# Order of the small row pieces in the second layer of a sparse expert kernel

## The chip, the cores and the metric

The kernel runs on one core of a Trainium2 chip. The metric is device time in microseconds (us) of one execution; lower is better. Three executions of the kernel before took 378.6, 380.12 and 380.73 us; the median, 380.12 us, is the time before.

## The reference

A linear attention without softmax is followed by a layer of eight experts. Each of 4608 rows (8 sequences of 576) has 512 features (8 heads of 64).

```python
kv  = einsum('bhsd,bhse->bhde', k, v)
out = einsum('bhsd,bhde->bhse', q, kv)
x   = out / sqrt(mean(out*out, -1) + 1e-6) * g_norm     # then (B,H,S,D) -> (4608, 512)

do_compute = x @ w_skip > 0                             # other rows are passed through
logits = x[do_compute] @ w_gate                         # 8 experts
e      = argmax(logits);  gate = softmax(logits)[e]
h      = maximum(x @ w1[e], 0)                          # 512 -> 1024
out    = x + gate * (h @ w2[e])                         # 1024 -> 512
```

All of it is in fp32. Each row that is computed goes through one expert alone, so the work is sparse: a row is gathered, taken through its expert's two layers, scaled and added to itself, and scattered back.

## The kernel before

**Stages.** The attention and the gating take roughly the first 130 us; the rest, up to 380 us, are the eight experts, ranked by their number of rows. Expert 0, the fullest, is begun beside the end of the attention. The others, 1 to 7, follow in one loop (`experts`), each with a first layer (`fast_1`) and a second layer (`fast_2`). Code behind a condition, for more rows than an expert has room for, isn't executed with these inputs.

**Rows and pieces.** The experts have room for 352, 352, 320, 288, 288, 288, 256 and 256 rows. Rows are cut into pieces of 128, and of what is left, 64 and 32. So from expert 1 on each has two whole blocks of 128 rows; expert 1 has a piece of 64 and one of 32 besides, expert 2 one of 64, experts 3, 4 and 5 one of 32, and experts 6 and 7 none.

**Seven products for two blocks.** The second layer of the two whole blocks is one matrix product, cut in 2 x 2 x 2 blocks and done with seven block products in place of eight (Strassen's method, in Winograd's form). Each product is four matmuls of 128 x 128 weights with 256 columns (line 1192); the profile shows each matmul as two rows, so a product is eight. Two PSUM banks, X and Y, hold the results, each in two halves, lo and hi:

1. X lo: block 0 of h with w2; ScalarE copies it out as p1 (`held`).
2. Y lo: sums of h with sums of w2; VectorE adds p1 to it (`add`, line 1196), then ScalarE copies it out as u (line 1202).
3. X hi: copied out by ScalarE as p5.
4. Y lo again, on top: it needs the add and the copy u of step 2 to be finished. VectorE then writes Y hi = Y lo + p5.
5. X lo again, on top.
6. X hi again, on top; VectorE adds u, and block 0's result is complete in X.
7. Y lo again, on top; block 1's result is complete in Y.

**Small pieces.** A piece of 64 or 32 rows goes the plain way (`layer_2`, line 1124). Its weights are only 64 or 32 columns wide, and two or four matmuls fill the array side by side: for each of the eight blocks f of 128 features there are 128/m matmuls of 512 m/128 columns, which write different partitions of one bank. A piece is in all 16 (m = 64) or 32 (m = 32) matmuls, twice that many rows in the profile. They accumulate in a bank of their own.

**Other work in the second layer.** VectorE makes, in twelve jobs given out by `do(work, n)`, what the next expert's first layer takes: four sums of its x (line 1140), then eight sums of its first-layer weights (line 1134). A finished piece goes to `put`, which is `result`: VectorE scales it with the gate and adds x (line 1336), and POOL issues an indirect DMA that scatters the rows (line 1339). In the first expert of the loop VectorE also has ten small instructions of a count of rounds and row tables ahead of these jobs.

**What sets the order.** Every engine's order is the order of the program text (`tc.manual_schedule`); no planner moves anything. Waits between engines come from the tiles' dependencies. PSUM banks come from a ring of seven (`bank`), claimed in program order. Weights are loaded on SP's queue, one expert's first and second layer (2 MB each) behind the other, into two sets of buffers; the load for expert r + 2 starts when expert r's weights were last read. Gathers and scatters are on POOL's queue; the gathers of expert r + 2 are issued at the start of expert r.

Of the kernel before, what the change touches and what calls it, by code (L numbers as in the profile page):

```python
# [17 lines left out]
def kernel(  # L18
# [58 lines left out]
    FC = F // 128  # L77
# [154 lines left out]
    for a in range(2):  # L232
        r = slice(a * 64, (a + 1) * 64)
# [215 lines left out]
    qTs, q8s, ops, rss, halves, lgs, xbs = {}, {}, {}, {}, {}, {}, {}  # L449
# [541 lines left out]
    with tc.tile_pool(name="wpool_b", bufs=1, reuse_waits="tile") as wpool_b, \  # L991
# [6 lines left out]
        def bank():  # L998
            return ps_b.tile([P, 512], FP32, tag="bank", name="bank")
# [116 lines left out]
        def layer_2(r, ht, piece, yps=None, fs=range(FC)):  # L1116

            off, m = piece[0:2]
            n = DM * m // P
            ht = ht if callable(ht) else (lambda f, all=ht: all[:, f, :])  # L1120
            yps = yps or bank()
            for f in fs:
                for q in range(P // m):
                    nc.tensor.matmul(out=yps[q * m:(q + 1) * m, 0:n], lhsT=ht(f)[:, off:off + m],  # L1124
                                     rhs=w_sb[r][1][:, f, q * n:(q + 1) * n],
                                     start=(f == 0), stop=(f == FC - 1), skip_group_check=True)
            return yps
# [15 lines left out]
        HF, HD = FC // 2, DC // 2  # L1143
# [40 lines left out]
        def do(work, n=None):  # L1184
            n = len(work) if n is None else min(n, len(work))
            for job in work[:n]:
                job()
            del work[:n]

        def product(out, k, lhsT, rhs, start):  # L1190
            for i in range(k):
                nc.tensor.matmul(out=out, lhsT=lhsT(i), rhs=rhs(i), start=start and i == 0,  # L1192
                                 stop=i == k - 1, skip_group_check=True)

        def add(to, x, y):
            nc.vector.tensor_tensor(out=to, in0=x, in1=y, op=ALU.add)  # L1196

        def held(x, tag):

            n = x.shape[-1]  # L1200
            t = ffn.tile([P, 256], FP32, tag=tag, name=tag)[:, 0:n]
            nc.scalar.copy(out=t, in_=x)  # L1202
            return t
# [61 lines left out]
        def fast_2(r, ht, rest, work, put, part=None):  # L1265

            w2, s, t = w_sb[r][1], sums.pop((r, "h")), sums.pop((r, "w2"))
            lo, hi = slice(0, HM), slice(HM, DM)

            def h(j, m):  # L1270
                return lambda f: ht[:, j * HF + f, m * P:(m + 1) * P]

            def hs(i):
                return lambda f: s[:, i, f, :]

            def w(j, ds):
                return lambda f: w2[:, j * HF + f, ds]

            def ws(i):
                return lambda f: t[:, i, f, :]  # L1280

            halves = [(piece, fs) for piece in rest for fs in (range(HF), range(HF, FC))]
            ys = {}

            def aside():
                if halves:
                    piece, fs = halves.pop(0)
                    if piece not in ys:  # L1290
                        ys[piece] = bank()
                    layer_2(r, ht, piece, ys[piece], fs)
                    if fs.stop == FC:
                        put(piece[0:2], ys[piece])

            X, Y = bank(), bank()
            product(X[:, lo], HF, h(0, 0), w(0, lo), True)
            p1 = held(X[:, lo], "p1")
            do(work, 4)
            product(Y[:, lo], HF, hs(1), ws(1), True)  # L1300
            add(Y[:, lo], Y[:, lo], p1)
            u = held(Y[:, lo], "u")
            do(work, 2)
            product(X[:, hi], HF, hs(0), ws(0), False)
            p5 = held(X[:, hi], "p5")
            do(work, 2)
            aside()
            product(Y[:, lo], HF, h(0, 1), ws(2), False)
            add(Y[:, hi], Y[:, lo], p5)
            if part:  # L1310
                part(1, 1, Y)
            do(work, 2)
            aside()
            product(X[:, lo], HF, h(1, 0), w(1, lo), False)
            do(work, 2)
            aside()
            product(X[:, hi], HF, hs(2), w(1, hi), False)
            add(X[:, hi], X[:, hi], u)
            put((0, P), X)
            aside()  # L1320
            product(Y[:, lo], HF, h(1, 1), ws(3), False)
            if part:
                part(1, 0, Y)
            else:
                put((P, P), Y)
            while halves:
                aside()
            do(work)

        def result(piece, yps, xg, tables, group):  # L1330
# [52 lines left out]
        def experts(pieces, widths, srcs, xt, ht, yps0, tables, group):  # L1383

            for r in range(E):
# [36 lines left out]
                if r == 0:  # L1422
                    if yps0 is None:
                        gather_all(2, pieces, *srcs)
                    ys = [bank() for _ in todo]
                    for fs in (range(HF), range(HF, FC)):
                        for piece, y in zip(todo, ys):
                            layer_2(r, ht, piece, y, fs)
                    do(beside, 4)
                    for piece, y in zip(todo, ys):  # L1430
                        result(piece, y, xgs[r], tables, group)
                    do(beside)
                else:
                    if yps0 is not None and r == 1:
                        rnd_i = rounds()
                    if yps0 is not None and r == E - 1:
                        n_rounds.append(nc.values_load(rnd_i[0:1, 0:1], min_val=1,
                                                       max_val=ROUNDS + 1))
                    of = {piece[0:2]: piece for piece in todo}
                    part = None  # L1440
                    if yps0 is not None and r == 1:
                        two = half_rows(tables[0][0])
                    if yps0 is not None and r == E - 1:
                        part = lambda c, half, y: half_result(c, half, y, xgs[r], two,
                                                              tables[0][1], group)
                    fast_2(r, ht, todo[2:], beside,
                           lambda key, y: result(of[key], y, xgs[r], tables, group), part)
# [134 lines left out]
```

## Time and profile before

| | us |
|---|---|
| median of three executions | 380.12 |
| profiled execution, in all | 381.81 |
| its span, first to last instruction | 380.0 |
| TensorE matmul busy | 365.3 (96%) |
| TensorE weight loads busy | 313.2 (82%) |
| VectorE busy | 245.1 (64%) |
| ScalarE busy | 142.3 (37%) |
| POOL busy | 124.2 (33%) |
| the seven products and the first layers, line 1192, share of the chain | 44% |
| small pieces, line 1124, share of the chain | 9% |

The granted TensorE clock is 0.999 of full speed throughout. In rows of the profile, "PE" is a matmul and "PEld" a weight load, which overlaps matmuls; "DVE" is VectorE, "ACT" ScalarE. A row in order of time gives start, length, engine, line, operation, output and inputs, shapes, and the number of merged instructions; the time in brackets is how long the engine was idle before and what ended it. [...] successive matmuls overlap, and it is the distance of their starts that counts. In the chain, and among the waits, "issue" is time in which an engine waited for nothing that the profile shows. A row of a table by stretches gives the stretch, its length, then the busy time (and number) of PE, PEld, DVE, ACT and POOL in it, the granted clock, and the DMA engines' share and GB/s. A row of waits gives who waited for whom, the time in total, how often, and the longest.

### The profile page before, as it was taken

What the parts mean: (1) busy time and instruction counts of PE and PEld (TensorE: products, weight loads), DVE (VectorE), ACT (ScalarE), POOL (GpSimd) and SP (SyncE); (2) the same over time, 40 slices, a digit from 0 to 9 for tenths busy, and PEclk for the clock granted to TensorE, in tenths of its full rate; (3) what the DMA queues carried; (4) which work ended last, traced back from release to release, by engine and by line L of the source; (5) the groups of instructions that cost most, each with busy time, mean ns of one, the idle gap of its engine ahead of it and who ended that gap; (6) DMA issues with size and microseconds to landing.
All of it is one profiled execution on the core that took longest, in us unless ns stands there. A gap on an engine that the chain in (4) does not pass through costs nothing.

```text
span 380.0 us, 9623 instructions
## 1 busy us (share of the span) xinstructions
PE 365.3 (96%) x3848; PEld 313.2 (82%) x3848; DVE 245.1 (64%) x626; ACT 142.3 (37%) x383; POOL 124.2 (33%) x195
## 2 busy tenths in 40 slices
PE   8999999999988998999999999999999999999994
PEld 4688797898977857779869987988988998998983
DVE  3344458667787961666756665875876876877831
ACT  2366676676774301214402430430440430431410
POOL 7025467655668544223013302212201211202003
PEclk9999999999999999999999999999999999999999
DMA  8999999996487738966516462672662762800001
GB/s 292 393 390 389 403 402 398 403 352 205 136 296 207 216 92 281 394 203 237 194 62 201 144 223 57 232 257 68 239 213 87 261 194 92 273 3 28 29 1 52
DMA packets 32039, 81.70 MB, mean 215 GB/s; under 512 B 2474, under 2 KB 2482, under 8 KB 31988
## 3 DMA queue, kind: packets, MB, share of 16 engines
q1 hardware_dynamic: 28176, 69.47, 52.1%
q0 software_dynamic: 3792, 11.53, 8.9%
q8 instruction: 32, 0.52, 0.6%
q14 instruction: 19, 0.16, 0.1%
q10 hardware_dynamic: 20, 0.02, 0.0%
HBM read 66.80 MB, written 14.48 MB: 214 GB/s over the span
## 4 chain that ended last, share of the span: by engine, by line
PE 84%; issue 6%; DVE 3%; ACT 3%; POOL 2%; DMA 1%; POOLq 0%; DVEq 0%; ACTq 0%
PE bank L1192 44%; PE bank L1124 9%; PE o_ps L496 6%; PE sum_ps L379 5%; PE bank L1112 4%; PE q_ps L460 3%; PE g_ps L393 2%; PE q_ps L170 2%; PE bank L1093 2%; DMA xg<-out_dram,src 1%; DVE rs L518 1%; DVE xl L537 1%; ACT sq L510 1%; PE q_ps L814 1%; PE g_ps L411 1%
## 5 line engine op out<-in xcount | busy, mean ns | idle before, releaser
L1202 ACT COPY p<-bank 128x128 f32<-128x128 f32 (+6 forms) x70 | 20.8, 297 | 100.3 <-PE bank L1192 89.3
L1192 PE MATMUL bank<-xt,w 128*128 128x128 f32 (+5 forms) x336 | 55.5, 288 | 0.1
L567 POOL TENSOR_TENSOR xb<-xl,g_b 128x512 f32<-128x512 f32 x36 | 44.4, 1234 | 32.5 <-DVE rs L532 30.6
L1192 PEld LDWEIGHTS bank<-xt,w 128*128 128x128 f32 x336 | 47.0, 190 | 2.0 <-DVE bank L1196 1.5
L1196 DVE TENSOR_TENSOR bank<-bank,p 128x128 f32<-128x128 f32 (+6 forms) x70 | 23.6, 337 | 37.1 <-PE bank L1192 36.0
L1192 PE MATMUL bank<-xs,s 128*128 128x128 f32 (+5 forms) x224 | 36.7, 289 | 0.0
L496 PE MATMUL o_ps<-kvd,qT 128*128 128x146 f32 x240 | 35.8, 290 | 1.0 <-ACT kvd L415 0.7
L1339 POOL DMA_INDIRECT out_dram<-xg,arows x9 | 10.0, 1112 | 78.7 <-DVE xg L1336 77.8
L518 DVE TENSOR_REDUCE rs<-sq 128x8 f32<-128x512 f32 x36 | 24.6, 682 | 16.2 <-ACT sq L510 16.0
L1124 PE MATMUL bank<-w,ht 128*32 128x128 f32 (+2 forms) x436 | 34.5, 319 | 0.0
L496 PEld LDWEIGHTS o_ps<-kvd,qT 128*128 128x128 f32 x240 | 31.6, 188 | 2.0 <-ACT kvd L415 1.5
L1192 PEld LDWEIGHTS bank<-xs,s 128*128 128x128 f32 x224 | 31.1, 190 | 1.0 <-ACT p L1202 0.8
L1339 POOL DMA_INDIRECT out_dram<-xg,rows x14 | 13.9, 994 | 53.2 <-DVE xg L1336 42.7
L1124 PEld LDWEIGHTS bank<-w,ht 128*32 128x32 f32 (+2 forms) x436 | 18.8, 120 | 13.2 <-issue 10.9
L537 DVE TENSOR_TENSOR xl<-o_ps,rs 128x584 f32<-128x584 f32 x34 | 26.1, 767 | 4.5 <-DVE rs L532 0.5
L1192 PE MATMUL bank<-t,ht 128*128 128x256 f32 x112 | 27.1, 385 | 0.0
L1192 PE MATMUL bank<-w,ht 128*128 128x256 f32 x112 | 27.1, 384 | 0.0
L1084 POOL DMA_INDIRECT xg<-out_dram,src x14 | 14.4, 1026 | 37.2 <-DMA out_dram<-xg,rows 13.9
L379 PE MATMUL sum_ps<-v,k 64*64 64x64 f32 x1152 | 25.6, 228 | 0.6 <-issue 0.6
L510 ACT ACTIVATE sq<-o_ps 128x512 f32<-128x512 f32 x34 | 20.3, 596 | 15.0 <-PE o_ps L496 14.5
L379 PEld LDWEIGHTS sum_ps<-v,k 64*64 64x64 f32 x1152 | 21.7, 140 | 4.7 <-issue 2.1
L1192 PE MATMUL bank<-t,hs 128*128 128x256 f32 x112 | 25.3, 379 | 0.0
(217 smaller groups left out, 680.5 us busy)
## 6 DMA issues: line engine op xcount, KB each, us to landing
w<-in_moe_w_dram SPq DMA_DIRECT2D x16, 2048.0 KB, 7.9
k<-in_k_dram SPq DMA_DIRECT2D x16, 576.0 KB, 9.7
v<-in_v_dram SPq DMA_DIRECT2D x16, 576.0 KB, 12.0
q<-in_q_dram SPq DMA_DIRECT2D x16, 576.0 KB, 9.2
out_dram<-xb SPq DMA_DIRECT2D x29, 256.0 KB, 4.4
out_dram<-xb POOLq DMA_DIRECT2D x7, 256.0 KB, 5.5
xg<-out_dram,src POOLq DMA_INDIRECT x16, 3.5
out_dram<-xg,rows POOLq DMA_INDIRECT x16, 7.1
```

The lines of the kernel that those rows point to most:

```text
L379: nc.tensor.matmul(out=sum_ps[w * 64:(w + 1) * 64, a, u, :], lhsT=kt[r, 2 * u + w, c, :], rhs=vt[r, 2 * u + w, c, :], start=(c == 0), stop ...
L496: nc.tensor.matmul(out=ps[:, w, 0:2 * PK].rearrange("p (r k) -> p r k", r=2)[:, :, cols], lhsT=qT[:, w, a, :], rhs=kvds[b % KVD][:, u, w, ...
L510: nc.scalar.activation(out=sq[:, :, :, :], in_=heads(ps, G, G + 2 * D), func=ACT.Square)
L518: nc.vector.tensor_reduce(out=rs[:, :, :], in_=sq[:, :, :, :].rearrange("p x y (a d) -> p x (y a) d", a=2), axis=AX.X, op=ALU.add)
L537: nc.vector.tensor_tensor(out=xl[:, :, :, :].rearrange("p x y (a k) -> p x (y a) k", a=2), in0=ps[:, :, 0:2 * PK].rearrange("p x (h k) -> ...
L567: late.append((lambda: nc.gpsimd.tensor_tensor(out=xb[:, :, 4 * u * D:(4 * u + 4) * D].rearrange("p r (w x) -> p r w x", w=2), in0=xl[:, : ...
L1112: nc.tensor.matmul(out=hps[:, cols], lhsT=w_sb[r][0][:, dc, f * P:(f + 1) * P], rhs=xt[:, dc, cols], start=(dc == 0), stop=(dc == DC - 1))
L1124: nc.tensor.matmul(out=yps[q * m:(q + 1) * m, 0:n], lhsT=ht(f)[:, off:off + m], rhs=w_sb[r][1][:, f, q * n:(q + 1) * n], start=(f == 0), s ...
L1192: nc.tensor.matmul(out=out, lhsT=lhsT(i), rhs=rhs(i), start=start and i == 0, stop=i == k - 1, skip_group_check=True)
L1196: nc.vector.tensor_tensor(out=to, in0=x, in1=y, op=ALU.add)
L1202: nc.scalar.copy(out=t, in_=x)
L1339: ins = nc.gpsimd.indirect_dma_start(out=cut_rows(m)[:, :], out_offset=bass.IndirectOffsetOnAxis(ap=rows[:, col:col + 1], axis=0), in_=x, ...
```

## The change

Before, each small piece was computed in two halves, four blocks f each. `aside()` took the next half, and stood at four places: between products 3 and 4, 4 and 5, 5 and 6, 6 and 7. Expert 1 used all four, the experts with one piece the first two. Afterwards all small pieces stand between products 6 and 7, each whole, one behind the other; `put` of each follows its last matmul, and so comes after block 0's. One of VectorE's twelve jobs, the last of the four x sums, moves from ahead of the add of product 2 to behind it. The first layers, expert 0, and the number and shapes of all instructions stay. Experts 6 and 7 have no small pieces: for expert 6 only the place of the x sum changes, for expert 7 nothing.

```diff
-            halves = [(piece, fs) for piece in rest for fs in (range(HF), range(HF, FC))]
-            ys = {}
-
-            def aside():
-                if halves:
-                    piece, fs = halves.pop(0)
-                    if piece not in ys:
-                        ys[piece] = bank()
-                    layer_2(r, ht, piece, ys[piece], fs)
-                    if fs.stop == FC:
-                        put(piece[0:2], ys[piece])
-
             X, Y = bank(), bank()
             product(X[:, lo], HF, h(0, 0), w(0, lo), True)
             p1 = held(X[:, lo], "p1")
-            do(work, 4)
+            do(work, 3)
             product(Y[:, lo], HF, hs(1), ws(1), True)
             add(Y[:, lo], Y[:, lo], p1)
             u = held(Y[:, lo], "u")
-            do(work, 2)
+            do(work, 3)
             product(X[:, hi], HF, hs(0), ws(0), False)
             p5 = held(X[:, hi], "p5")
             do(work, 2)
-            aside()
             product(Y[:, lo], HF, h(0, 1), ws(2), False)
             add(Y[:, hi], Y[:, lo], p5)
             if part:
                 part(1, 1, Y)
             do(work, 2)
-            aside()
             product(X[:, lo], HF, h(1, 0), w(1, lo), False)
             do(work, 2)
-            aside()
             product(X[:, hi], HF, hs(2), w(1, hi), False)
             add(X[:, hi], X[:, hi], u)
             put((0, P), X)
-            aside()
+            for piece in rest:
+                put(piece[0:2], layer_2(r, ht, piece))
             product(Y[:, lo], HF, h(1, 1), ws(3), False)
             if part:
                 part(1, 0, Y)
             else:
                 put((P, P), Y)
-            while halves:
-                aside()
             do(work)
```

## The prediction

> **What bounds the kernel now.** I read the page's chain of work first, because a change of order matters only on the engine that sets the end.
>
> ```profile
> PE 84%; issue 6%; DVE 3%; ACT 3%; POOL 2%; DMA 1%; POOLq 0%; DVEq 0%; ACTq 0%
> PE bank L1192 44%; PE bank L1124 9%; PE o_ps L496 6%; PE sum_ps L379 5%; PE bank L1112 4%; PE q_ps L460 3%; PE g_ps L393 2%; PE q_ps L170 2%; PE bank L1093 2%; DMA xg<-out_dram,src 1%; DVE rs L518 1%; DVE xl L537 1%; ACT sq L510 1%; PE q_ps L814 1%; PE g_ps L411 1%
> ```
>
> TensorE carries the chain. The two first lines are the two that the change reorders: L1192 are the seven products, L1124 the small pieces. Next I asked whether TensorE waits for anybody there (waits of its weight loads, 184 to 350 us).
>
> ```profile
> PEld bank L1124 <- issue: 4.0, 12, 0.3
> PEld bank L1192 <- issue: 3.1, 12, 0.4
> PEld bank L1192 <- DVE bank L1196: 1.1, 5, 0.3
> PEld bank L1192 <- ACT p L1202: 0.6, 4, 0.2
> ```
>
> Little of it is for other engines; 24 times, some 7 us in all, the next weights wait for "issue", which is nothing that the profile names. The order of time shows where: expert 3 (one 32-row piece), TensorE alone.
>
> ```profile
> 250.28 1.89 PE L1192 MATMUL bank<-w,ht 128*128 128x256 f32 x8
> 252.01 3.62 PE L1192 MATMUL bank<-t,hs 128*128 128x256 f32 x16
> 255.56 1.08 PE L1124 MATMUL bank<-w,ht 128*32 128x128 f32 x32
> 256.57 1.99 PE L1192 MATMUL bank<-t,ht 128*128 128x256 f32 x8
> 258.50 1.08 PE L1124 MATMUL bank<-w,ht 128*32 128x128 f32 x32
> 259.51 1.99 PE L1192 MATMUL bank<-w,ht 128*128 128x256 f32 x8
> ```
>
> Expert 6 has no small piece, so it already runs the seven products in the order of the new kernel:
>
> ```profile
> 338.69 3.62 PE L1192 MATMUL bank<-t,hs 128*128 128x256 f32 x16
> ...
> 340.69 0.43 DVE L1196 TENSOR_TENSOR bank<-bank,p 128x256 f32<-128x256 f32 x1 [1.02 <-PE bank L1192]
> ...
> 341.15 0.37 ACT L1202 COPY u<-bank 128x256 f32<-128x256 f32 x1 [1.89 <-DVE bank L1196]
> 341.93 1.70 PEld L1192 LDWEIGHTS bank<-t,ht 128*128 128x128 f32 x8
> 342.14 1.89 PE L1192 MATMUL bank<-t,ht 128*128 128x256 f32 x8
> ```
>
> Start to start a product there takes 1.73 us. In expert 3 a product between halves takes 1.93 (256.57 to 258.50): each visit to a small piece also slows its neighbours. The stretches from the first product of the second layer to the first of the next expert price this:
>
> ```profile
> 184.53:203.19 18.66, 18.66 (x155) 14.06 (x153) 11.84 (x33) 1.95 (x6) 2.21 (x2) 1.00 0.38 125
> 219.77:236.01 16.24, 16.24 (x91) 12.60 (x89) 9.79 (x21) 1.96 (x6) 1.24 (x2) 1.00 0.40 143
> 250.28:264.79 14.51, 14.51 (x122) 12.11 (x121) 9.62 (x21) 2.38 (x7) 1.24 (x2) 1.00 0.45 153
> 336.96:349.05 12.09, 12.09 (x58) 10.65 (x57) 9.26 (x20) 1.89 (x5) 0.03 (x1) 1.00 0.00 1
> ```
>
> The first number is the length, the next is PE busy: TensorE fills every one. Experts 1, 2, 3 and 6, in that order; 4 and 5 give 14.50 each. So the small pieces cost 6.57, 4.15, 2.42, 2.41 and 2.41 us over the bare 12.09.
>
> [...] In the single records of expert 3, in-mode starts of a product are 0.216 us apart; the last start before a piece is 0.309 before the piece's first one, 0.093 more. [...] the 32-wide matmuls do start in groups of four, within 0.02 us, a group every 0.109 us (64-wide: pairs every 0.216).
>
> **The change, part by part.**
>
> *Fewer visits.* The number of matmuls is the same; what falls away is mode switches. A 32-row half is 8 groups, 8 x 0.109 = 0.87 us, but costs 2.42 / 2 = 1.21: a visit's switches cost 0.335. A 64-row half is 8 pairs, 8 x 0.216 = 1.73, and costs 4.15 / 2 = 2.075: 0.345. Expert 1 confirms it: 2 x 1.73 + 2 x 0.87 = 5.20, plus 2 x 0.345 + 2 x 0.335 = 1.36, gives 6.56 against 6.57. Experts 3, 4, 5 drop one visit each of two: 3 x 0.335 = 1.0 us. Expert 2 drops one: 0.345.
>
> *Expert 1* has four visits, and afterwards goes from products to the 64-row piece, to the 32-row piece, to the product: three switches for eight. A direct switch from 64 to 32 is in no trace of before. From the records [...] a slower start in the new mode: 0.06 for 64, 0.04 for 32, 0.10 for 128 columns. Three switches make 0.28 + 0.20 = 0.48 for 1.36: 0.88 saved. Bounds: the direct switch free, 1.02; each piece paying a whole visit, 0.68. I take 0.88. A gain from it beyond that has no source, since no matmul goes.
>
> *The cover between products 3 and 4.* Product 4 adds to the half bank that product 2 wrote; VectorE must have added to it and ScalarE copied it to u. With the half piece gone, product 3's 1.73 us alone covers this. Expert 6 shows it enough: u is done at 341.52, the weights start at 341.93. Experts 2 to 5: in expert 3 u ends 254.85, product 4's weights would be due at 255.25; expert 4 is tightest, 284.52 against 284.57. Cost nothing; behind the waiting weight load all later matmuls would queue, so each us late there is a us of the end.
> Expert 1 is another matter. VectorE comes late there, since ten small instructions of the rounds count and the row tables run first; u ends at 189.98, and product 4's weights would be due at 189.50. Moving one of the four x sums (0.41 us from start to start) behind the add brings u to 189.58: 0.08 late, of which the 0.2 us between a weight load and its matmul may hide all. I take 0.05 us; 0 to 0.15. Left in place, it would have been 0.4.
>
> *The moved x sum* costs VectorE nothing: in experts 2 to 6 VectorE idles before that add (1.02 us in expert 6). Its taker is the next expert's first layer, over 8 us later. The two w sums behind it shift by the same 0.41; VectorE is busy 9.3 of 12.09 us in expert 6, done in time.
>
> *Scaled results and scatters.* Block 0's result, with its scatter, now goes first; the small ones follow, then block 1's. Each is one VectorE instruction (0.34 to 0.75) and one POOL issue (about 1.0). Between the end of the last small piece and block 1's result lie product 7 and its way, 1.73 + 0.2 + 0.75, so POOL is free again. The gathers of expert r + 2 stand behind block 1's scatter on POOL as before and are taken a whole expert (29 us) later. Cost nothing.
>
> *Banks, weights on SP's queue.* The pieces' banks are claimed in the same order, and come round seven claims later, some 6 us into the next first layer. The next second-layer weights load when TensorE last read the old ones: product 6 before (issue at 263.26), the end of the piece now. Both are one product before the stage's end, and 7.9 us of landing have an expert's time. Experts 6 and 7 keep their TensorE order.
>
> Sum: 1.0 + 0.345 + 0.88 - 0.05 = 2.18 us. The profiled execution has a span of 380.0 us and took 381.81 in all; after, 377.8 and 379.6. The median of the three runs is 380.12, near the span; the same 2.18 off it gives **377.9 us**, ratio 0.994. What a measurement of this kernel can tell from no change is about 0.5%, 1.9 us: the forecast lies only just beyond.
>
> **Rivals.**
> *Slower: long runs of small matmuls starve.* Place: the second half of each 32-row piece. [...] It decides from 44 ns per matmul (0.55 us in each of four experts eats the gain); 59 ns makes it slower by 0.5%. Against it stands a run of 80 matmuls in 64-by-64 tiles[...], with (1.40 - 0.23) / 79 = 15 ns each:
>
> ```profile
> 21.00 1.40 PE L379 MATMUL sum_ps<-v,k 64*64 64x64 f32 x80
> ```
>
> [...] Product 4 late in every expert with pieces, as expert 4's tight 0.05 us and expert 1's backlog suggest: 0.2 us in five experts leaves 1.2 of the gain, 379.0. Against it: 0.4 us to spare in experts 3 and 6.
>
> *Nothing saved.* The 0.33 belongs to the start of each accumulating half (its first weights), not to the visit, or the other experts' loads set the pace behind TensorE: 380.1. Against it: the product after a half also lengthens, and TensorE is busy in 100% of these stretches.
>
> **How the numbers follow.** Forecast 0.70, of which 0.10 falls inside the 0.5% by the scatter of medians (the three runs spread over 2.1 us); the wait 0.13, of which 0.01 beyond it; nothing saved 0.08; slower 0.09. Faster 0.61, within 0.30, slower 0.09. The forecast's own bounds are a saving of 1.9 to 2.4, 377.7 to 378.2; a median's scatter widens it to 376.7. To leave no more than 2 in 10 out, the range goes up through the wait and most of "nothing": 376.7 to 379.9.
>
> **What would show it.** After: stretches of the second layer of about 17.8 us in expert 1, 15.9 in expert 2, 14.17 in 3 to 5, and 12.09 still in 6; one row of 64 matmuls in 32 columns, 1.95 us long, a group every 0.109; products 1 to 6 at 1.73. [...] if the load of product 4's weights waits for ScalarE's u, the cover was too thin. The forecast is wrong if a direct switch from 64 to 32 columns costs more than a visit, or if time comes back in the first layers, which should not change.

## The result, and the profile after

The median of the new kernel is 378.11 us (20 runs, 376.23 to 379.63) against 380.13 us for the kernel before (20 runs, 378.6 to 382.03). The ratio is 0.9944, with a 95% interval of 0.9932 to 0.9956: about 2.1 us, or 0.56%, faster. The forecast was 377.9 us. The profiled execution of the new kernel has a span of 376.7 us.

The chain of work on the new kernel's page has the same main owners as before (a 2% share of the loads of v, in the attention, is new):

```profile
PE 82%; issue 6%; DMA 3%; ACT 3%; DVE 3%; POOL 2%; SPq 0%; POOLq 0%; DVEq 0%; ACTq 0%
PE bank L1192 44%; PE bank L1124 9%; PE o_ps L496 6%; PE sum_ps L379 4%; PE bank L1112 4%; PE q_ps L460 3%; PE g_ps L393 2%; DMA v<-in_v_dram 2%; PE bank L1093 2%; PE q_ps L814 1%; DMA xg<-out_dram,src 1%; DVE rs L518 1%; DVE xl L537 1%; ACT sq L510 1%; PE g_ps L411 1%
```

TensorE still carries the chain, with 82% of it. The waits of TensorE's weight loads between 184 and 350 us:

```profile
PEld bank L1124 <- issue: 1.4, 4, 0.4
PEld bank L1192 <- issue: 1.2, 5, 0.4
PEld bank L1192 <- DVE bank L1196: 1.0, 5, 0.2
PEld bank L1192 <- ACT p L1202: 0.8, 5, 0.2
PEld bank L1124 <- PE bank L1192: 0.7, 2, 0.3
PEld bank L1192 <- ACT u L1202: 0.2, 1, 0.2
```

Where 24 loads waited 7.1 us for "issue", 9 now wait 2.6 us; two more carry the name of the product before them instead (0.7 us). In the single records these 11 stand at the 11 changes of weight width that are left, three in expert 1 and two in each of experts 2 to 5. One new line stands at the end: one load waits 0.15 us (rounded to 0.2) for the copy u.

TensorE in order of time, expert 3 of the new kernel:

```profile
248.02 1.89 PE L1192 MATMUL bank<-w,ht 128*128 128x256 f32 x8
249.75 3.62 PE L1192 MATMUL bank<-t,hs 128*128 128x256 f32 x16
253.21 1.89 PE L1192 MATMUL bank<-t,ht 128*128 128x256 f32 x8
254.93 1.89 PE L1192 MATMUL bank<-w,ht 128*128 128x256 f32 x8
256.66 1.89 PE L1192 MATMUL bank<-w,hs 128*128 128x256 f32 x8
258.48 1.95 PE L1124 MATMUL bank<-w,ht 128*32 128x128 f32 x64
260.36 1.99 PE L1192 MATMUL bank<-t,ht 128*128 128x256 f32 x8
```

Products 1 to 5 follow each other at 1.73 us: in the single records a matmul is 0.379 us long, and the next starts 0.216 us after it, so that two overlap. Product 6 takes 1.82 (256.66 to 258.48): its last start and the piece's first one are 0.309 us apart and not 0.216, as at each such change in the kernel before. The piece is one row of 64 matmul records (32 matmuls with two records each), 1.95 us long; they start in groups of four, 0.02 us from the first to the fourth, a group every 0.109 us. Product 7 starts slowly, with 0.32 us between its first two starts, and takes 1.83. The stretches of the second layer, of experts 1, 2, 3 and 6, in the columns shown before (stretch, length, busy times):

```profile
183.49:201.28 17.79, 17.79 (x155) 14.37 (x154) 11.85 (x33) 1.96 (x5) 3.00 (x3) 1.00 0.43 146
217.85:233.75 15.90, 15.90 (x91) 12.78 (x90) 9.79 (x21) 1.97 (x6) 1.97 (x2) 1.00 0.47 157
248.02:262.19 14.17, 14.17 (x122) 12.25 (x121) 9.71 (x21) 1.95 (x6) 1.80 (x2) 1.00 0.44 155
333.59:345.68 12.09, 12.09 (x58) 10.65 (x57) 9.27 (x20) 1.90 (x5) 0.03 (x1) 1.00 0.00 1
```

From the single records they are 0.86 us shorter in expert 1, 0.35 in expert 2, and 0.335 in each of experts 3, 4 and 5; expert 6 is unchanged. That is 2.22 us. The spans differ by 3.3 us. The rest is not of the change: 0.1 us lies in expert 5's first layer, and 1.05 us ahead of expert 1, in code that is the same in both; from expert 7's first product to the end the new kernel takes 0.08 us longer. In the profiled executions of all kernels of this study that keep this code expert 1's second layer starts between 181.7 and 185.1 us (why it varies, the runs don't show), so two spans can differ by 3 us before the changed lines are reached. Below, effects are therefore read from the stretches, which repeat within 0.02 us, and the times are given beside them.

### The profile page after: what moved, and what is told of

Same layout as the page of the kernel before. It is cut to its first block, busy times and chain, and to the rows that moved or that the text cites. A ratio compares the mean times of both kernels' runs of the same rounds, so it can differ in the third digit from the quotient of the medians.

```text
span 376.7 us, 9624 instructions
## 1 busy us (share of the span) xinstructions
PE 362.9 (96%) x3848; PEld 314.8 (84%) x3848; DVE 244.3 (65%) x626; ACT 142.9 (38%) x383; POOL 122.7 (33%) x195
## 4 chain that ended last, share of the span: by engine, by line
PE 82%; issue 6%; DMA 3%; ACT 3%; DVE 3%; POOL 2%; SPq 0%; POOLq 0%; DVEq 0%; ACTq 0%
PE bank L1192 44%; PE bank L1124 9%; PE o_ps L496 6%; PE sum_ps L379 4%; PE bank L1112 4%; PE q_ps L460 3%; PE g_ps L393 2%; DMA v<-in_v_dram 2%; PE bank L1093 2%; PE q_ps L814 1%; DMA xg<-out_dram,src 1%; DVE rs L518 1%; DVE xl L537 1%; ACT sq L510 1%; PE g_ps L411 1%
## 5 line engine op out<-in xcount | busy, mean ns | idle before, releaser
L567 POOL TENSOR_TENSOR xb<-xl,g_b 128x512 f32<-128x512 f32 x36 | 43.5, 1211 | 32.5 <-DVE rs L532 30.6
L1124 PE MATMUL bank<-w,ht 128*32 128x128 f32 (+2 forms) x436 | 33.2, 318 | 0.0
L379 PE MATMUL sum_ps<-v,k 64*64 64x64 f32 x1152 | 24.7, 223 | 0.8 <-issue 0.6
L379 PEld LDWEIGHTS sum_ps<-v,k 64*64 64x64 f32 x1152 | 20.9, 134 | 4.7 <-issue 1.7
L1192 PEld LDWEIGHTS bank<-t,ht 128*128 128x128 f32 x112 | 20.8, 190 | 3.9 <-issue 1.2
```

The costliest lines, as they stand in the source:

```text
L379: nc.tensor.matmul(out=sum_ps[w * 64:(w + 1) * 64, a, u, :], lhsT=kt[r, 2 * u + w, c, :], rhs=vt[r, 2 * u + w, c, :], start=(c == 0), stop ...
L567: late.append((lambda: nc.gpsimd.tensor_tensor(out=xb[:, :, 4 * u * D:(4 * u + 4) * D].rearrange("p r (w x) -> p r w x", w=2), in0=xl[:, : ...
```

## The experiments

Lengths of the second layer's stretches, in us, first product to first matmul of the next expert, from the single records of each profiled execution. The ratios are those on record, with their 95% intervals; each sets a kernel against executions of the kernel before taken with it, so it isn't the quotient of two times of this table:

| kernel | expert 1 | 2 | 3, 4, 5 each | time, ratio to before |
|---|---|---|---|---|
| before | 18.66 | 16.24 | 14.51 | 380.13 |
| new | 17.79 | 15.89 | 14.17 | 378.11, 0.9944 (0.9932 to 0.9956) |
| halves back to back | 18.08 | 15.89 | 14.17 | 377.04, one execution |
| whole, but early | 17.78 | 15.89 | 14.17 | 379.98, one execution |
| 4 and 2 jobs | 18.19 | 15.89 | 14.17 | 378.16, 0.9931 (0.9908 to 0.9954) |
| halves, 3 and 3 jobs | 18.66 | 16.24 | 14.51 | 379.90, 0.9996 (0.998 to 1.0012) |
| quarters | 19.23 | 16.94 | 15.18 | 383.93, 1.0098 (1.0073 to 1.0123) |
| 6 and 0 jobs | 19.39 | 15.89 | 14.17 | 379.66, 0.9993 (0.9973 to 1.0012) |
| fewer switches | 17.63 | 15.89 | 14.17 | 377.35, 0.9923 (0.9902 to 0.9944) |
| new, second time | 17.78 | 15.89 | 14.17 | 377.75, 0.9946 (0.992 to 0.9973) |
| fewer switches, second time | 17.64 | 15.89 | 14.17 | 377.36, 0.9934 (0.9913 to 0.9955) |

The theory was that each visit to a small piece costs its switches of mode, that is, its changes between weights of 128, 64 and 32 columns. The rivals were that each accumulating half pays for its own start, that the place or the moved sum brings the gain, and that a wait for u takes it back.

**Halves back to back.** The pieces stand between products 6 and 7, but in halves.

```diff
-            for piece in rest:
-                put(piece[0:2], layer_2(r, ht, piece))
+            ys = [bank() for _ in rest]
+            for fs in (range(HF), range(HF, FC)):
+                for piece, y in zip(rest, ys):
+                    layer_2(r, ht, piece, y, fs)
+            for piece, y in zip(rest, ys):
+                put(piece[0:2], y)
```

> The new kernel, but between products 6 and 7 the pieces are taken in halves again: first halves of all pieces, then second halves. Experts 2 to 5 then compute two halves back to back with no change of mode between them; expert 1 goes 64, 32, 64, 32 columns. If a switch of mode is what costs (theory of the prediction): stretches of experts 2 to 5 stay at 15.89 and 14.17 us, and expert 1 grows from 17.79 by two switches, 2 x 0.093 + 0.06 + 0.04 = 0.29, to 18.08. If each accumulating half pays for its start, whatever the mode (rival 'nothing saved', whose second half is only covered elsewhere in the new kernel): 16.24 and 14.51 as before the change, and expert 1 near 18.66.

Stretches of experts 1, 2 and 3:

```profile
181.80:199.88 18.08, 18.08 (x154) 14.22 (x153) 11.85 (x33) 1.96 (x6) 2.67 (x3) 1.00 0.41 137
216.46:232.35 15.89, 15.89 (x90) 12.77 (x89) 9.79 (x21) 1.96 (x6) 1.97 (x2) 1.00 0.46 156
246.63:260.80 14.17, 14.17 (x123) 12.25 (x121) 9.71 (x21) 1.95 (x6) 1.81 (x2) 1.00 0.47 155
```

A half alone costs nothing here: experts 2 and 3 are as short as with whole pieces, 15.89 and 14.17 us. Two more switches in expert 1 cost 0.29 us, as worked out. The rival "nothing saved" falls with it: the price is of the switch, not of the half. A change of bank isn't it either: products go from bank X to bank Y and back at 1.73 us.

**Whole, but early.** The loop over the whole pieces is moved up.

```diff
             p5 = held(X[:, hi], "p5")
             do(work, 2)
+            for piece in rest:
+                put(piece[0:2], layer_2(r, ht, piece))
             product(Y[:, lo], HF, h(0, 1), ws(2), False)
...
-            for piece in rest:
-                put(piece[0:2], layer_2(r, ht, piece))
             product(Y[:, lo], HF, h(1, 1), ws(3), False)
```

> The new kernel, but the whole pieces stand between products 3 and 4, where the first half stood before, and product 4 so has its long cover again. If only the number of mode switches counts: the same stretches as the new kernel, 17.79, 15.89 and 14.17 us. If the place between products 6 and 7 has a part in the gain (results of block 0 leaving earlier[...]), the stretches grow, by up to 0.3 us each.

Stretches of experts 1, 2 and 3:

```profile
185.07:202.85 17.78, 17.78 (x155) 14.46 (x153) 11.94 (x33) 1.97 (x6) 2.05 (x3) 1.00 0.38 132
219.43:235.32 15.89, 15.89 (x91) 12.77 (x89) 9.80 (x21) 1.96 (x6) 1.05 (x2) 1.00 0.40 144
249.60:263.77 14.17, 14.17 (x123) 12.24 (x122) 9.72 (x21) 1.95 (x6) 1.05 (x2) 1.00 0.45 155
```

They are those of the new kernel, within 0.02 us. The place has no part in the gain of the switches. In expert 1 both pieces, 5.49 us of work in the new kernel, stand here ahead of product 4, whose weights so don't wait for u, and the stretch is the 0.02 us shorter; the x sum might have stayed where it was, which no run shows. The time of the one execution, 379.98 us, would have said otherwise; its expert 1 began latest of all executions, at 185.1 us, 1.6 us after the new kernel's.

**4 and 2 jobs.** The new kernel with the fourth x sum ahead of the add again.

```diff
-            do(work, 3)
+            do(work, 4)
             product(Y[:, lo], HF, hs(1), ws(1), True)
             add(Y[:, lo], Y[:, lo], p1)
             u = held(Y[:, lo], "u")
-            do(work, 3)
+            do(work, 2)
```

> The new kernel with the four x sums ahead of the add again, as before the change. Prediction's theory: product 4's weights wait for ScalarE's copy u in expert 1 alone, u ending 0.5 us after they are due, of which 0.1 to 0.2 hides: expert 1's stretch 18.1 to 18.2 us for 17.79, others unchanged, the time 0.3 to 0.4 us longer than the new kernel, ratio to before about 0.9955. If the cover were too thin in general, experts 3 and 4 would grow too. If the order of that sum doesn't matter: 17.79.

Expert 1's stretch is 18.19 us, 0.40 more; the others stay. In order of time, expert 1 of this kernel, and then of the new one:

```profile
187.80 0.42 DVE L1196 TENSOR_TENSOR bank<-bank,p 128x256 f32<-128x256 f32 x1
...
188.26 0.37 ACT L1202 COPY u<-bank 128x256 f32<-128x256 f32 x1 [2.77 <-DVE bank L1196]
...
188.68 1.59 PEld L1192 LDWEIGHTS bank<-t,ht 128*128 128x128 f32 x8 [0.55 <-ACT u L1202]
188.69 1.99 PE L1192 MATMUL bank<-t,ht 128*128 128x256 f32 x8 [0.15 <-ACT u L1202]
```

```profile
187.70 0.42 DVE L1196 TENSOR_TENSOR bank<-bank,p 128x256 f32<-128x256 f32 x1
188.03 0.48 DVE L1140 TENSOR_TENSOR xs<-xt,xs 128x320 f32<-128x320 f32 x1
188.16 0.37 ACT L1202 COPY u<-bank 128x256 f32<-128x256 f32 x1 [2.37 <-DVE bank L1196]
...
188.58 1.59 PEld L1192 LDWEIGHTS bank<-t,ht 128*128 128x128 f32 x8 [0.15 <-ACT u L1202]
188.67 1.91 PE L1192 MATMUL bank<-t,ht 128*128 128x256 f32 x8
```

Each time the weights of product 4 wait for u: 0.55 us here, 0.15 in the new kernel, where the first matmul starts on time and product 4 takes 0.02 us more. The moved sum is so worth 0.40 us, in expert 1 alone. The measured time can't tell 0.4 us: the median is 378.16 us against the new kernel's 378.11, and the ratio, for which 0.9955 was expected, has an interval from 0.9908 to 0.9954.

**Halves, 3 and 3 jobs.** The kernel before with only the x sum moved.

```diff
-            do(work, 4)
+            do(work, 3)
             product(Y[:, lo], HF, hs(1), ws(1), True)
             add(Y[:, lo], Y[:, lo], p1)
             u = held(Y[:, lo], "u")
-            do(work, 2)
+            do(work, 3)
```

> The kernel before with only the x sum moved behind the add (3 and 3 jobs), the halves where they stood. Prediction's theory: no effect, stretches 18.66, 16.24, 14.51 and 12.09 us, ratio to before 1.000 within its interval. If the moved sum, and not the pieces, brings part of the gain, the ratio is below 0.998 and the stretches shrink.

Ratio 0.9996 and the stretches of before. By itself the moved sum brings nothing; it only pays, 0.40 us, once the half piece that covered u is gone.

**Quarters.** Each piece in four visits, two blocks f each.

```diff
+            def quarter(i):
+                for piece in rest:
+                    if piece not in ys:
+                        ys[piece] = bank()
+                    layer_2(r, ht, piece, ys[piece], range(2 * i, 2 * i + 2))
+                    if i == 3:
+                        put(piece[0:2], ys[piece])
...
+            quarter(0)
             product(Y[:, lo], HF, h(0, 1), ws(2), False)
...
+            quarter(1)
             product(X[:, lo], HF, h(1, 0), w(1, lo), False)
...
+            quarter(2)
             product(X[:, hi], HF, hs(2), w(1, hi), False)
...
-            for piece in rest:
-                put(piece[0:2], layer_2(r, ht, piece))
+            quarter(3)
             product(Y[:, lo], HF, h(1, 1), ws(3), False)
```

> The new kernel with each piece cut in quarters of two blocks f, one visit at each of the four places between products 3 and 7; where expert 1 has two pieces, both quarters are taken one behind the other. This doubles the visits of before. If each visit costs its switches: experts 3 to 5 12.09 + 1.75 + 4 x 0.335 = 15.18 us each, expert 2 12.09 + 3.46 + 4 x 0.345 = 16.93, expert 1 12.09 + 5.20 + 4 x 0.48 = 19.21; in all 3.3 us above before, 5.4 above the new kernel, time about 383.4, ratio to before 1.0085. If more visits are covered by the weight loads that TensorE takes ahead, less than half of that.

Stretches of experts 1, 2 and 3:

```profile
183.61:202.85 19.24, 19.24 (x155) 13.79 (x154) 11.83 (x33) 1.97 (x6) 1.51 (x2) 1.00 0.33 116
219.42:236.36 16.94, 16.94 (x90) 12.29 (x89) 9.70 (x21) 1.97 (x6) 1.02 (x1) 1.00 0.36 132
250.66:265.83 15.17, 15.17 (x122) 11.84 (x121) 9.61 (x21) 1.95 (x6) 0.80 (x1) 1.00 0.42 148
```

19.23, 16.94 and 15.18 against 19.21, 16.93 and 15.18: with one, two and four visits expert 3 takes 14.17, 14.51 and 15.18, a straight line of 0.335 us a visit. The time, 383.93 us (ratio 1.0098), is the largest change of the study.

**6 and 0 jobs.** The cover of u worn thin: `do(work, 6)` ahead of product 2, none behind the copy u.

```diff
-            do(work, 3)
+            do(work, 6)
             product(Y[:, lo], HF, hs(1), ws(1), True)
             add(Y[:, lo], Y[:, lo], p1)
             u = held(Y[:, lo], "u")
-            do(work, 3)
```

> The new kernel with the four x sums and two w sums ahead of the add (6 and 0 jobs), to see what the cover between products 3 and 4 is worth. VectorE's two w sums take 1.2 us from start to start. Prediction's theory: expert 1's u ends near 191.2 on the clock of before against 189.5, so product 4 is 1.5 to 1.7 us late there; expert 3 0.1 to 0.2 late; experts 2, 4, 5 and 6 within 0.1, since VectorE idled ahead of the add. In all 1.6 to 1.9 us, and the gain nearly gone: 379.7 to 380.0, ratio to before 0.999 to 1.000. If the load of product 4's weights doesn't really wait for u, nothing changes.

Expert 1's second layer in order of time:

```profile
186.30 1.28 DVE L1134 TENSOR_TENSOR s<-w 128x512 f32<-128x512 f32 x2
187.50 0.42 DVE L1196 TENSOR_TENSOR bank<-bank,p 128x256 f32<-128x256 f32 x1
...
188.38 1.59 PEld L1192 LDWEIGHTS bank<-t,ht 128*128 128x128 f32 x8 [1.75 <-ACT u L1202]
188.38 2.00 PE L1192 MATMUL bank<-t,ht 128*128 128x256 f32 x8 [1.35 <-ACT u L1202]
```

Two w sums stand before the add, and the weights wait 1.75 us. Expert 1 grows by 1.60 us, as forecast, which leaves 0.62 us of the 2.22 in the stretches. The ratio is 0.9993, not to be told from the kernel before: this one wait takes most of the gain. Expert 3 was expected 0.1 to 0.2 us late and lost nothing: u ends there at 252.47 us, 0.3 before the weights load at 252.79. So in experts 2 to 6, whose stretches are all unchanged, the cover bears even this.

**Fewer switches.** The new kernel with two more switches out.

```diff
+            wide = 32 if r == 1 and m == 64 else m
             for f in fs:
-                for q in range(P // m):
-                    nc.tensor.matmul(out=yps[q * m:(q + 1) * m, 0:n], lhsT=ht(f)[:, off:off + m],
+                for q, lo in itertools.product(range(P // m), range(0, m, wide)):
+                    nc.tensor.matmul(out=yps[q * m + lo:q * m + lo + wide, 0:n],
+                                     lhsT=ht(f)[:, off + lo:off + lo + wide],
                                      rhs=w_sb[r][1][:, f, q * n:(q + 1) * n],
...
-                    for fs in (range(HF), range(HF, FC)):
-                        for piece, y in zip(todo, ys):
-                            layer_2(r, ht, piece, y, fs)
+                    for piece, y in zip(todo, ys):
+                        layer_2(r, ht, piece, y)
```

> The new kernel with two more switches taken out: expert 0's 32-row piece whole behind the whole block (one visit less, 0.335 us), and expert 1's 64-row piece computed with weights of 32 columns, four at a time with 256 columns each, in the mode of the 32-row piece (one switch less; the 64-row start of 0.06 becomes the 32-row one of 0.04, 0.15 us in all). If switches are all that counts: expert 1's stretch 17.64 us, expert 0's whole block and piece 9.18 - 0.335 = 8.84, time 0.5 us below the new kernel, ratio to before 0.993. If smaller weights cost more in the 64-row piece (twice the number of matmuls, 128 rows in a line), expert 1's stretch grows by up to 1 us and the time is that of the new kernel or above.

The stretches of expert 0's whole block and piece, and of expert 1's second layer:

```profile
155.95:164.80 8.85, 8.85 (x83) 4.56 (x81) 7.47 (x14) 0.90 (x3) 3.25 (x3) 1.00 0.93 365
182.64:200.27 17.63, 17.63 (x186) 14.28 (x185) 11.84 (x33) 1.96 (x6) 3.00 (x3) 1.00 0.41 148
```

In the new kernel they are 9.18 and 17.79: 0.33 and 0.16 less. TensorE alone, in expert 1 of this kernel, and then of the new one, the pieces and product 7:

```profile
193.10 5.41 PE L1125 MATMUL bank<-w,ht 128*32 128x256 f32 x128
198.44 2.00 PE L1194 MATMUL bank<-t,ht 128*128 128x256 f32 x8
```

```profile
193.96 5.56 PE L1124 MATMUL bank<-w,ht 128*64 128x256 f32 x96
199.45 1.99 PE L1192 MATMUL bank<-t,ht 128*128 128x256 f32 x8
```

Both pieces are one row here, 128 matmul records, and take 5.34 us to the start of product 7; in the new kernel they take 5.49, 3.60 for the 64-row piece and 1.88 for the other. Twice the number of smaller weight loads costs nothing here: four records start every 0.216 us, where two did. To see whether the time follows, both kernels were measured again, on one chip.

> The new kernel itself once more, beside the next one on the same chip. By its stretches 2.2 us below before: ratio 0.994, 378.0 us.

> The kernel with two more switches taken out once more, to see whether the 0.48 us less of its stretches is also seen in the time. If so: 0.3 to 0.7 us below the new kernel, ratio to before about 0.993; if something outside the stretches gives it back, the same time as the new kernel.

The new kernel: 377.75 us, ratio 0.9946 (0.992 to 0.9973). With fewer switches: 377.36 us, 0.9934 (0.9913 to 0.9955). The median is lower by 0.4 us here, and by 0.76 in the first measurements (377.35 against 378.11), but the intervals overlap. That the stretches are 0.48 us shorter is shown; that the time is shorter than the new kernel's is likely, and not shown by the times alone. Against the kernel before it is clearly faster.

## Why the prediction was right

- **Price of a visit.** 0.335 us for 32 columns and 0.345 for 64, from the stretches of before. Experts 3, 4 and 5 gave back 0.335 each, expert 2 0.348. The quarters and the halves back to back show that the switch is what is paid. What the runs show is this price; what the array does in that time they don't show. The prediction's split of it is rough at one end: it takes the 0.093 us by which 0.309 exceeds 0.216 for every switch (0.28 for expert 1's three, with 0.20 for the slower starts), and from 32 columns back to 128 the records show 0.114 (0.223 for 0.109); the sum by visit is right.
- **Expert 1's direct switch from 64 to 32 columns**, which no trace of before held. The estimate was a saving of 0.88 (0.68 to 1.02), with 0.05 of wait against it. The stretch gave 0.86, of which the wait had taken 0.02: the whole pieces early, without a wait, gave 0.88. In the records the last 64-column start and the first 32-column one are 0.309 us apart, as from a product to a piece, and the 32-row piece then takes 1.88, as in expert 3.
- **The cover between products 3 and 4.** Expected to hold in experts 2 to 5: it does, in all of them product 4 starts 3.45 us after product 2, as in expert 6. In expert 1 0.05 us was set aside; the weights wait 0.15, which costs 0.02. Left in place, the fourth x sum was priced at 0.4, and measured 0.40.
- **Work costed at nothing.** The moved sum, scatters, banks and weight loads left no trace on TensorE: the first layers of experts 2 to 7 are unchanged within 0.02 us, but for expert 5's (0.1 us shorter; it has the shorter length in the kernel before with 3 and 3 jobs as well; in the kernel before one load waited there 0.31 us for an add of VectorE, 0.21 in the new one, and why that add came later once isn't known).
- **The sum.** 2.18 us predicted, 2.22 in the stretches, 2.1 by the ratio. The forecast lay just beyond the 0.5%, and so did the measurement. That the median, 378.11 us, came within 0.2 us of the forecast is in part luck: the second time the same kernel's was 377.75.
- **The rival of starved runs** doesn't occur: the 64 matmul records of a whole piece take 1.88 us to the next product, which is a half's 1.01 and 0.87 for the other half, with a group of four every 0.109 us to the end, 27 ns a record. The rates at which the prediction lets this rival decide, 44 and 59 ns, are estimates from its 0.87 us a half, its gain of 2.18 us and the 0.5%; that a longer run would slow to them no trace showed. In the last experiment's row of 128 the last 64 keep that pace too. The wait as rival is real as a mechanism, at 1.6 us in the 6 and 0 version, but only in the expert whose VectorE comes late.

## What to carry to other kernels

Where TensorE is busy without a gap, look at the distance of starts at each change of weight width (here 0.309 us for 0.216): work with weights of another width is then better done in one visit, which here cost 0.335 to 0.345 us each, and two widths that stand side by side may share the narrower one, as 64 and 32 columns do here for 0.16 us. A piece of other work between dependent products is cover as well as cost (without it expert 1's product 4 waited 0.55 us for u, and 0.15 with the x sum moved); before it is taken out, find the one place where the engine that feeds the next product is late, and reorder that engine. For gains of half a per cent, compare the changed stretch and not one execution's time.

## What the runs showed that was not expected

Part of a weight load's wait was free here, 0.13 us. In expert 1 product 4's weights waited 0.15, 0.55 and 1.75 us in three kernels, and the stretch was 0.02, 0.42 and 1.62 us longer than with the whole pieces early, where they don't wait for u: the wait less 0.13 us each time. The prediction took each us of that wait for a us of the end; beyond the 0.13 this is what the three stretches show. Expert 1's 64-row piece runs as fast with weights of 32 columns as with 64: four records start together every 0.216 us with 32, and two with 64.
